# Expert-choice logits of a fused attention and mixture-of-experts kernel: rows stationary against gate weights stationary

## The chip, the cores and the metric

The kernel runs on one core of one Trainium2 chip. The metric is device microseconds (us) of one execution, as the median of several runs. All times below are in us unless marked ns.

## What is computed

Four batches of eight heads, 576 tokens and 64 elements a head go through an attention that keeps only scores within `tau` of the row's largest. The heads of a token are put side by side into a row of 512, which gives 2304 rows. Each row chooses one of 8 experts by the largest of 8 logits, the expert takes at most `capacity` rows in the order of the rows, and the row goes through that expert's two layers:

```python
x = attn_out.transpose(0, 2, 1, 3).reshape(2304, 512)
logits = x @ w_gate                       # 512 x 8
expert_idx = np.argmax(logits, axis=1)
probs = softmax(logits); gate_w = probs[i, expert_idx[i]]
disp[e, counts[e]] = x[i]                 # while counts[e] < capacity, rows in order
h = np.maximum(disp @ w1, 0); y = h @ w2  # w1: 512 x 1024, w2: 1024 x 512 for each expert
out[i] = gate_w[i] * y[expert_idx[i], pos[i]]
```

The change touches only `x @ w_gate` for the first 512 tokens of each batch.

## The kernel before

**Stages.** The attention runs over 16 pairs of heads (`s` in 0 to 15; `HH` = 4 pairs make one batch). Per pair TensorE (PE) computes the scores twice (`emit_s`, whose row maxima VectorE takes at L819, and `emit_d`, transposed, for the exponentials), ScalarE takes the exponentials (L880) and rounds them to f16 (L850), VectorE masks them (L884), GpSimd makes the low halves (L854), and PE multiplies by the values (`emit_av`, L900 and, for the 64 tail tokens of each head, L912) into the PSUM bank `xo`. GpSimd writes the scaled rows into `xr` (L950; tails into `xrt`).

**The gate.** When a pair's rows are there, `emit_xturn` transposes them, two blocks of 128 tokens at a time, into columns 0 to 255 of the PSUM bank `gp` (L955), and `emit_xturned` copies them with ScalarE into `xgt4` (L960). `xgt4` is carved out of the memory of `w2b`, and that is its name in the profile. It holds, for each of the four pairs `c` of a batch, 128 features by 512 tokens in f32. After the last pair of a batch `emit_logits` (L966) multiplies: for each of the 4 blocks of 128 tokens and each `c`, the 128x128 block of rows is the stationary operand and the 128x8 slice of the gate's weights `wg` moves. That is 16 matmuls a batch, and since the profile shows each f32 matmul as two passes with a weight load each, 32. The 64 tail tokens have their own path (`emit_turn` L981, `emit_turned` L987, `emit_logit` L997). Then `emit_gate1`, `emit_choice`, `emit_rank`, `emit_meta` and `emit_gate2` (L1021 to L1086) find expert and position on VectorE, with a few small matmuls, and GpSimd scatters the rows to DRAM (L1092).

**Experts.** The first rows of each expert ("early" tiles) are gathered before the last batch's rows are scattered, and the rest ("late") after it. Their layers are L377/L384 and L423, with weights loaded as `ws` and split into two f16 halves (L307/L314, L309 to L312).

**What sets the order.** No engine's order is written by hand. Every step is a task `T(key, engine, duration, function, dependencies, priority)`, and `Plan.run` simulates the engines with the written durations and emits the steps in the order that comes out. A task's duration and its dependencies thus move other tasks too. The logits of a batch were one task on PE, written as 1800 ns.

Of the kernel before, what the change touches and what calls it, by code (L numbers as in the profile page):

```python
# [14 lines left out]
AF = mybir.ActivationFunctionType  # L15
ALU = mybir.AluOpType
AX = mybir.AxisListType
# [3 lines left out]
P = 128  # L21
# [9 lines left out]
def view(ap, dims, offset=0):  # L31
    return bass.AP(tensor=ap.tensor, offset=ap.offset + offset, ap=[ap.ap[0]] + [list(d) for d in dims])
# [138 lines left out]
def attention_moe_kernel(ctx: ExitStack, tc: tile.TileContext, q, k, v, tau, w_gate, w1, w2, cap, out):  # L171
    nc = tc.nc
    B, H, S, D = q.shape
    NTOK, DM = out.shape
    E, _, F = w1.shape
    NJ = S // P
    TAIL = S - NJ * P
    NB = DM // P
# [27 lines left out]
    V = nc.vector  # L206

    def const_of(name, shape, dt=F32):
        return const.tile([P] + shape, dt, name=name)

    tau_t, g64, cap_f, cap_e = (const_of(n, [1]) for n in ("tau_t", "g64", "cap_f", "cap_e"))
    cap_i = const_of("cap_i", [2], I32)
    wg = const_of("wg", [NB, E])
    ntau = const_of("ntau", [1])
    ones, tri, tri2, ident16 = (const_of(n, [P], F16) for n in ("ones", "tri", "tri2", "ident16"))
    ident = const_of("ident", [P])
# [20 lines left out]
    for i, t0, m, pattern, base in (  # L237
# [4 lines left out]
        nc.gpsimd.iota(hs_i[:, i, t0:t0 + m], pattern=pattern, base=base, channel_multiplier=0)  # L242
    V.memset(ones, 1.0)
    V.memset(cum, 0.0)
    V.memset(zero, 0.0)
    nc.gpsimd.affine_select(
        out=tri, in_=ones, pattern=[[1, P]], base=0, channel_multiplier=-1, compare_op=ALU.is_gt, fill=0.0
    )
    for i in range(2):
# [6 lines left out]
        out=row_e, in0=desc, scalar1=-float(NTOK), scalar2=float(E * NTOK), op0=ALU.mult, op1=ALU.add  # L256
# [3 lines left out]
        out=more_e, in0=desc, scalar1=float(E - NP), scalar2=float(HP), op0=ALU.is_gt, op1=ALU.mult  # L260
# [4 lines left out]
        out=half[:, 1:2], in0=half[:, 0:1], scalar=-float(HP), in1=tok_l, op0=ALU.mult, op1=ALU.add  # L265
    )
    for t in (slice(0, NF), slice(NL, SLOTS)):
        V.tensor_scalar(out=hslot[:, 0, t], in0=hslot[:, 0, t], scalar1=half[:, 0:1], scalar2=None, op0=ALU.add)
    V.tensor_scalar(
        out=hslot[:, 2], in0=hslot[:, 0], scalar1=float(HP), scalar2=half[:, 1:2], op0=ALU.mult, op1=ALU.add  # L270
# [51 lines left out]
    psum = ctx.enter_context(tc.tile_pool(name="psum", bufs=1, space=PSUM))  # L322
    ps_x, ps_g = (psum.tile([P, 512], F32, name=n) for n in ("xo", "gp"))
# [119 lines left out]
    tb = {}  # L443
# [203 lines left out]
    if True:  # L647
# [14 lines left out]
        HH = H // 2  # L662
# [5 lines left out]
        def part(shape, dt=F32, i=1):  # L668
            n = 2 if dt == F32 else 1
            for d in shape:  # L670
                n *= d
            at[i] += n
            assert at[i] <= WB - 512
            v = wb[i][:, WB - at[i]:WB - at[i] + n]
            dims, step = [], 1
            for d in reversed(shape):
                dims.insert(0, [step, d])
                step *= d
            return view(v.bitcast(F32) if dt == F32 else v, dims)
# [5 lines left out]
        xgt4 = part([NB, NM])  # L685
# [273 lines left out]
        def emit_xturned(s, i):  # L959
            nc.scalar.activation(out=xgt4[:, s % HH, i * 2 * P:(i + 1) * 2 * P], in_=ps_g[:, 0:2 * P], func=AF.Copy)  # L960

        def emit_logits(b):
            gps[b, 0] = ps_g
            for j in range(NJ):
                for c in range(NB):
                    nc.tensor.matmul(  # L966
                        out=ps_g[:, 2 * P + j * E:2 * P + (j + 1) * E], lhsT=xgt4[:, c, j * P:(j + 1) * P], rhs=wg[:, c, :],
                        start=(c == 0), stop=(c == NB - 1),
                    )

        xgt, gps = {}, {}

# [16 lines left out]
        def emit_logit(b, j):  # L989
            gp = gps[b, j - j % NJ]  # L990
            xg = xgt.pop((b, j))
            o = 2 * P + (j % NJ) * E
            for c in range(NB):
                for z in range(1 if j < NJ else 2):
                    m = slice(0, P) if j < NJ else slice(z * TAIL, (z + 1) * TAIL)
                    x = xg[:, c] if j < NJ else xg[:, c % 2, c // 2 * TAIL:(c // 2 + 1) * TAIL]
                    nc.tensor.matmul(  # L997
                        out=gp[m, o:o + E], lhsT=x, rhs=wg[:, c, :], start=(c == 0), stop=(c == NB - 1)
                    )

        def bc(x, g, n):
# [122 lines left out]
        def emit_first2():  # L1124
# [10 lines left out]
        plan = Plan()  # L1135

        NU = 9 * NPR
        NQ = B * (NJ + 1)
# [3 lines left out]
            scat=13.88, ld=-34, lv=-26, sc=-25, hi=-24, lo=-22, tk=-20, s=-14, sj=0.8, m=-9, d=0, dj=1.8, e=-1.5, p=-1, h=.5, l=1, vs=-8, av=9, avx=4,  # L1142
# [4 lines left out]
        T, J = plan.add, plan.join  # L1147

        def last(kind, n, *more):
            return [(kind, n, *more)] if n >= 0 else []  # L1150
# [10 lines left out]
        T(("tau",), "V", 140, emit_tau, [("ltau",)], -60)  # L1161
        T(("lcap",), "S", 475, lambda: nc.sync.dma_start(out=cap_i, in_=cap.partition_broadcast(P)), [("s", 1, 3)], 20, dma=60, kind="load")
        T(("cap",), "V", 280, emit_cap, [("lcap",)], 25)
        T(("lwg",), "S", 475, lambda: nc.sync.dma_start(out=wg, in_=w_gate.rearrange("(c p) e -> p c e", p=P)), [("s", 1, 2)], 20, dma=230, kind="load")

        CUT = 2 * NJ + 3
        FIRST = 2
# [4 lines left out]
        for s in range(NPR):  # L1172
            b, a = divmod(s, HH)
            u = 9 * s
            scaled = s >= FIRST
            for is_q in (False, True):
                n = "q" if is_q else "k"
# [33 lines left out]
            for c in (0, 5, 1, 2, 3, 4):  # L1211
                pr = u + PR["d"] + PR["dj"] * (c % 5)
                n = 5 * s + c
                if c < 5:
                    free = [("p", *divmod(n - 2, 5))] if n >= 2 else []
                    if c:
                        m = 4 * s + c - 1 - N32
# [8 lines left out]
                if 0 < c < 5:  # L1226
                    m = 4 * s + c - 1 - N16
                    uses = [("av", m // 4, m % 4 // 2, j) for j in range(NJ)] if m >= 0 else []
                    T(("h16", s, c), "A", 1030, partial(emit_h16, s, c), [("p", s, c)] + uses, pr + PR["h"])
                    e = "V" if c in BY_V else "G"  # L1230
# [16 lines left out]
            t = u + PR["xt"] + PR["av"]  # L1247
# [7 lines left out]
                continue  # L1255
            n = u + 8
            t = n + PR["xt"]
            T(("logit", b, 0), "P", 1800, partial(emit_logits, b), [("xb", s, 1), ("lwg",)] + last("gate2", b - 1, NJ), t)
            qi = b * (NJ + 1) + NJ
            T(("ta", qi), "P", 216, partial(emit_turn, b, NJ, 0), [("xm", s - i, 2) for i in range(HH)] + [("xb", s, 1)], t)  # L1260
            T(("tb", qi), "A", 264, partial(emit_turned, b, NJ, 0), [("ta", qi)] + last("logit", b - 1, NJ), t, kind="psum")
            T(("logit", b, NJ), "P", 756, partial(emit_logit, b, NJ), [("tb", qi), ("gate2", b, 0)], t)
            for i in (0, NJ):
                t = n + PR["gate"]
# [21 lines left out]
        b = B - 2  # L1286
# [15 lines left out]
        def at(n):  # L1302
            return NU + PM["B0"] + n * PM["SL"]

        g = B - 1
        plan.urgent |= {(n, g, NJ) for n in ("gate1", "gexp", "choice", "rank", "meta", "gate2")} | {("scat", g, NJ, 0)} | {(n, NQ - 1) for n in ("ta", "tb")} | {("logit", g, 0), ("logit", g, NJ)}
        if PR["urg"] > 0:
            plan.urgent |= {(n,) for n in ("tot", "most", "left", "cnt", "cut", "alone", "lim", "base", "base2", "dv", "u", "w1", "w2")}
            plan.urgent |= {(n, 0) for n in ("ge", "pr", "sel", "row", "gix")}
# [26 lines left out]
        for i, t in enumerate((first, rest)):  # L1336
            m, p = t.stop - t.start, i / 2
# [29 lines left out]
        for t in range(NE, NS, GR):  # L1367
            m = min(GR, NS - t)
# [11 lines left out]
        for c in range(NCH):  # L1380
            ends = c == NCH - 1
            for i in range(2):
# [32 lines left out]
                for t in range(NS):  # L1415
                    early = t < NE and c == 0
                    n = NU + PR["early"] + t * PR["ej"] if early and i == 0 else at(pos)
                    o = (lambda p: n) if early and i == 0 else (lambda p: at(pos + PM[p]))
# [3 lines left out]
                    if i == 0:  # L1422
                        if c == 0:
                            xb = XB[t % len(XB)]
# [17 lines left out]
                        if t >= NE and (t % 2 or t == NS - 1):  # L1442
                            m = t % 2 + 1
# [3 lines left out]
                    else:  # L1447
# [3 lines left out]
                        e = "A" if c == 0 and t < NE else "V"  # L1451
# [74 lines left out]
```

## Time and profile before

| | |
|---|---|
| median of 3 runs | 625.91 (625.09 to 627.33) |
| the profiled execution's own time | 626.25 |
| its span, first to last instruction | 624.4 |
| mean granted TensorE clock | 0.959 |
| busy time in the span: PE, DVE, ACT, POOL | 556.9, 432.3, 383.3, 426.9 |

PE is TensorE, DVE is VectorE, ACT is ScalarE, POOL is GpSimd, PEld is PE's weight loads. A granted clock of 1.00 is 2.4 GHz and 0.50 is 1.2 GHz. Matmuls are pipelined and the ends of their rows are modelled, so what a group of them costs PE is read from its start to the start of the next. The four groups of logits start at 121.25, 198.46, 278.43 and 358.12; the first three lie inside the attention, the last one between attention and experts.

### The profile page before, as it was taken

The numbers are of one execution on the slowest core, as the hardware profiler recorded it, in microseconds if no ns is written. First come the engines' busy times: TensorE is split into PE (matmuls) and PEld (weight loads), VectorE is DVE, ScalarE is ACT, GpSimd is POOL, SyncE is SP. The second block draws the span as 40 slices with busy tenths as digits, with TensorE's granted clock in tenths as the row PEclk, the third lists the DMA queues.
The fourth block names the chain that finished last, engine by engine and source line by source line (L and its number), as shares of the span: only waits on it lengthen the run. The fifth ranks groups of instructions, "written<-read, shape, count | busy, mean of one in ns | idle before, by whom it ended". The sixth has DMA issues, their size and how long they took to land.

```text
span 624.4 us, 15985 instructions
## 1 busy us (share of the span) xinstructions
PE 556.9 (89%) x5990; PEld 378.3 (61%) x5990; DVE 432.3 (69%) x990; ACT 383.3 (61%) x523; POOL 426.9 (68%) x366
## 2 busy tenths in 40 slices
PE   0777999998999999999797895799999999999994
PEld 0234666765667666666566784665775577468652
DVE  4667988878886888886877869444555655555652
ACT  4359888878797688574467643448556645644410
POOL 5327887949887389772768536508788948886774
PEclk9989999989999899998798888989999999999997
DMA  5878777736677367662243845962579519861972
GB/s 152 193 174 166 135 149 138 152 95 156 152 171 137 58 172 133 116 87 49 77 141 99 296 160 157 223 157 77 203 194 220 173 67 222 207 202 61 232 185 100
DMA packets 171181, 94.26 MB, mean 151 GB/s; under 512 B 147027, under 2 KB 159383, under 8 KB 171098
## 3 DMA queue, kind: packets, MB, share of 16 engines
q1 hardware_dynamic: 157450, 50.47, 40.1%
q0 software_dynamic: 12352, 41.80, 20.8%
q8 instruction: 52, 0.85, 0.6%
q10 hardware_dynamic: 1296, 0.89, 0.4%
q14 instruction: 31, 0.25, 0.1%
HBM read 53.25 MB, written 10.24 MB: 102 GB/s over the span
## 4 chain that ended last, share of the span: by engine, by line
PE 60%; DVE 14%; DMA 9%; SPq 5%; ACT 4%; issue 4%; POOL 3%; ACTq 0%; POOLq 0%; DVEq 0%
PE b L384 10%; PE xo L900 9%; PE s L792 8%; PE d L792 7%; PE b L377 7%; PE xo L423 5%; PE gp L423 4%; PE b L423 4%; DVE w2b L884 3%; PE gp L966 2%; DMA out_dram<-latey,oix 2%; PE xo L912 2%; DVE mx L819 2%; SPq L733 2%; DMA qr<-in_q_dram 2%
## 5 line engine op out<-in xcount | busy, mean ns | idle before, releaser
L792 PE MATMUL s<-kT,qT 128*128 128x512 f16 (+2 forms) x576 | 99.5, 310 | 28.8 <-DMA kT<-kn 22.2
L819 DVE TENSOR_REDUCE mx<-s 128x1 f32<-128x512 f32 x144 | 94.4, 679 | 17.4 <-PE s L792 16.6
L792 PE MATMUL d<-qT,kT 128*128 128x512 f16 (+2 forms) x576 | 85.4, 302 | 6.0 <-DVE w2b L884 4.5
L384 PE MATMUL b<-w1b,latex 128*128 (+2 forms) x816 | 79.4, 274 | 5.3 <-DVE latex L359 3.6
L309 ACT ACTIVATE ws<-ws 128x1024 f32<-128x1024 f32 x48 | 50.5, 1051 | 51.1 <-DMA ws<-in_moe_w_dram 51.1
L384 PEld LDWEIGHTS <-latex 128*128 128x128 f16 (+1 forms) x816 | 62.3, 102 | 21.3 <-DVE latex L359 4.8
L792 PEld LDWEIGHTS <-qT 128*128 128x128 f16 (+1 forms) x640 | 39.7, 105 | 57.3 <-issue 25.7
L884 DVE SCALAR_TENSOR_TENSOR w2b<-d,ntau,w2b 128x1024 f32<-128x1024 f32 x56 | 71.0, 1276 | 3.6 <-ACT w2b L880 3.6
L854 POOL TENSOR_TENSOR p<-w2b,p 128x1024 f16<-128x1024 f32 x33 | 70.3, 2135 | 3.2 <-ACT p L850 2.8
L312 POOL TENSOR_TENSOR w2b<-ws,w2b 128x1024 f16<-128x1024 f32 x24 | 51.0, 2137 | 23.0 <-ACT w2b L310 22.8
L792 PEld LDWEIGHTS <-kT 128*128 128x128 f16 (+1 forms) x640 | 37.1, 102 | 47.7 <-issue 28.0
L312 POOL TENSOR_TENSOR w1b<-ws,w1b 128x1024 f16<-128x1024 f32 x24 | 51.3, 2141 | 20.6 <-ACT w1b L310 20.3
L880 ACT ACTIVATE w2b<-d 128x1024 f32<-128x1024 f32 x56 | 56.3, 1019 | 5.5 <-PE d L792 4.7
L900 PEld LDWEIGHTS <-p 128*128 128x128 f16 x1056 | 47.2, 103 | 14.8 <-issue 4.1
L377 PE MATMUL b<-earlyx,w1b 128*128 128x128 f16 x768 | 51.1, 228 | 5.4 <-DVE earlyx L359 5.2
L377 PEld LDWEIGHTS <-w1b 128*128 128x128 f16 x768 | 47.4, 102 | 12.8 <-issue 10.3
L900 PE MATMUL xo<-vH,p 128*128 128x65 f16 x704 | 49.9, 199 | 3.9 <-DVE rc L935 2.6
L423 PEld LDWEIGHTS <-lateh 128*128 128x128 f16 (+1 forms) x408 | 30.8, 103 | 33.6 <-issue 0.4
L296 POOL DMA_DIRECT2D ws<-in_moe_w_dram x50 | 37.3, 750 | 9.7 <-DVE w2b L314 7.3
L900 PE MATMUL xo<-vL,p 128*128 128x64 f16 x352 | 43.9, 197 | 0.0
L850 ACT ACTIVATE p<-w2b 128x1024 f16<-128x1024 f32 x33 | 34.8, 1055 | 6.1 <-DVE w2b L884 5.8
L310 ACT ACTIVATE w2b<-ws 128x1024 f16<-128x1024 f32 x24 | 25.4, 1057 | 20.9 <-PE gp L423 20.2
(231 smaller groups left out, 1225.6 us busy)
## 6 DMA issues: line engine op xcount, KB each, us to landing
ws<-in_moe_w_dram POOLq DMA_DIRECT2D x50, 512.0 KB, 5.1
ws<-in_moe_w_dram SPq DMA_DIRECT2D x14, 512.0 KB, 4.7
kr<-in_k_dram SPq DMA_DIRECT2D x15, 256.0 KB, 2.9
qr<-in_q_dram SPq DMA_DIRECT2D x14, 256.0 KB, 2.9
v<-in_v_dram SPq DMA_DIRECT2D x28, 128.0 KB, 3.2
qr<-in_q_dram ACTq DMA_DIRECT2D x2, 256.0 KB, 4.8
v<-in_v_dram POOLq DMA_DIRECT2D x4, 128.0 KB, 3.3
qT<-qn SPq DMA_TRANSPOSE x32, 4.7
```

Of the source, the lines that this page charges most:

```text
L296: eng.dma_start(out=t, in_=src)
L309: nc.scalar.activation(out=t, in_=t, func=AF.Copy, scale=W_SCALE)
L312: nc.gpsimd.tensor_tensor(out=dst[:, :, 1, :], in0=t, in1=dst[:, :, 0, :], op=ALU.subtract)
L377: nc.tensor.matmul(out=hp[:, f * P:(f + 1) * P], lhsT=wb[0][:, o:o + P], rhs=xT[t][:, xi], start=(d == 0 and z == 0), stop=(d == NB - 1 an ...
L384: nc.tensor.matmul(out=hp[m, 0:FC], lhsT=xT[t][:, xi, m], rhs=wb[0][:, bass.ds(r + (2 * d + wi) * FC, FC)], start=(d == 0 and z == 0), sto ...
L423: nc.tensor.matmul(out=yp[m], lhsT=h[:, o, hi, m], rhs=wb[1][:, bass.ds(r + wi * DM, DM)], start=(z == 0), stop=(z == len(ops) - 1),)
L792: nc.tensor.matmul(out=out, lhsT=l, rhs=r, start=(z == 0), stop=(z == 1), **kw)
L819: V.tensor_reduce(out=m[:, i, 0:1], in_=ps_s[i % 2], axis=AX.X, op=ALU.max)
L854: eng.tensor_tensor(out=p[:, 1], in0=p32_of(s, k), in1=p[:, 0], op=ALU.subtract)
L880: nc.scalar.activation(out=t, in_=d, func=AF.Exp, scale=sc_s)
L884: V.scalar_tensor_tensor(out=t, in0=d, scalar=ntau, in1=t, op0=ALU.is_ge, op1=ALU.mult)
L900: nc.tensor.matmul(out=ps_x[:, j * DV:j * DV + r.shape[-1]], lhsT=l, rhs=r, start=(z == 0), stop=(z == len(ops) - 1))
```

## The change

The operands are exchanged. For each half `h` of a batch (256 tokens), `emit_gated` makes the gate's slices stationary: `wg` is now 128 x 4 x 32, zero but for the 8 experts, and each `c` has a column tile of its own, 32 columns wide, with its output in 32 partitions of `gp`. The rows move, 256 columns at a time. The four parts of the sum then lie in four groups of partitions, tokens along the row. `emit_parts` copies them (128x256) back to SBUF on ScalarE, over `xgt4`'s first block. `emit_logits` adds the four parts and turns them in one matmul per 128 tokens, with the parts stationary and `pick` moving, a 128x8 matrix of 0 and 1. `pick` is made once from the identity; `wg` is filled with zeros once. The tail's transposes (`ta`) now wait for the second copy, since both use columns 0 to 255 of `gp`.

```diff
-    wg = const_of("wg", [NB, E])
+    wg = const_of("wg", [NB, P // NB])
+    pick = const_of("pick", [E])
...
+    V.memset(wg, 0.0)
...
-        def emit_logits(b):
+        def emit_gated(b, h):
             gps[b, 0] = ps_g
-            for j in range(NJ):
-                for c in range(NB):
-                    nc.tensor.matmul(
-                        out=ps_g[:, 2 * P + j * E:2 * P + (j + 1) * E], lhsT=xgt4[:, c, j * P:(j + 1) * P], rhs=wg[:, c, :],
-                        start=(c == 0), stop=(c == NB - 1),
-                    )
+            for c in range(NB):
+                r = slice(c * P // NB, (c + 1) * P // NB)
+                nc.tensor.matmul(
+                    out=ps_g[r, 0:2 * P], lhsT=wg[:, c, :], rhs=xgt4[:, c, 2 * h * P:2 * (h + 1) * P], start=True, stop=True
+                )
+
+        def emit_parts(b, h):
+            nc.scalar.activation(out=xgt4[:, 0, 2 * h * P:2 * (h + 1) * P], in_=ps_g[:, 0:2 * P], func=AF.Copy)
+
+        def emit_logits(b, h):
+            for j in (2 * h, 2 * h + 1):
+                nc.tensor.matmul(
+                    out=ps_g[:, 2 * P + j * E:2 * P + (j + 1) * E], lhsT=xgt4[:, 0, j * P:(j + 1) * P], rhs=pick,
+                    start=True, stop=True,
+                )
...
-                        out=gp[m, o:o + E], lhsT=x, rhs=wg[:, c, :], start=(c == 0), stop=(c == NB - 1)
+                        out=gp[m, o:o + E], lhsT=x, rhs=wg[:, c, 0:E], start=(c == 0), stop=(c == NB - 1)
...
+        T(("pick",), "V", 100, lambda: V.tensor_reduce(
+            out=pick, in_=view(ident[:, 0:E], [[1, E], [P // NB, NB]]), axis=AX.X, op=ALU.add), [("tau",)], 25)
...
-            T(("logit", b, 0), "P", 1800, partial(emit_logits, b), [("xb", s, 1), ("lwg",)] + last("gate2", b - 1, NJ), t)
+            for h in range(2):
+                T(("lgt", b, h), "P", 560, partial(emit_gated, b, h), [("xb", s, 1), ("lwg",)] + ([("lge", b, 0)] if h else []), t + h / 4)
+                T(("lge", b, h), "A", 370, partial(emit_parts, b, h), [("lgt", b, h)], t + h / 4, kind="psum")
+                T(("lgs", b, h), "P", 520, partial(emit_logits, b, h), [("lge", b, h), ("pick",)] + last("gate2", b - 1, NJ), t + h / 4)
+            J(("logit", b, 0), [("lgs", b, 0), ("lgs", b, 1)])
...
-            T(("ta", qi), "P", 216, partial(emit_turn, b, NJ, 0), [("xm", s - i, 2) for i in range(HH)] + [("xb", s, 1)], t)
+            T(("ta", qi), "P", 216, partial(emit_turn, b, NJ, 0), [("xm", s - i, 2) for i in range(HH)] + [("lge", b, 1)], t)
```

How the steps fall on the engines is shown at three places. In the changed kernel every line number is higher (`emit_gated` is L968, `emit_parts` L973, `emit_logits` L977).

PE at the logits of the first batch, before:

```order
L792 MATMUL s_145<-kT_181,qT_184 128x512
L966 MATMUL gp<-wg,w2b 128x8 x16
L981 MATMUL gp<-ident,xrt 128x128 x2
L792 LDWEIGHTS kT_183
L792 MATMUL gp<-qT_186,kT_183 64x64
```

The same place in the change, with the pieces that lie between:

```order
L968 MATMUL gp<-w2b,wg 32x256 x4
L794 LDWEIGHTS kT_185
L794 MATMUL gp<-qT_188,kT_185 64x64
...
L902 MATMUL xo<-v_170,w1b 128x65
L977 MATMUL gp<-pick,w2b 128x8 x2
L968 MATMUL gp<-w2b,wg 32x256 x4
L794 LDWEIGHTS qT_186
L794 MATMUL s_148<-kT_183,qT_186 128x512
...
L992 MATMUL gp<-ident,xrt 128x128 x2
L977 MATMUL gp<-pick,w2b 128x8 x2
```

The block of 16 has become four pieces, with one block of `emit_av` between the first two and two blocks and a pair of score matmuls between the last two. In all four batches the order is of this kind.

ACT at the same place, in the change (`w2b<-gp` at L962 is the last transposed block, at L973 the two new copies; `kn` and `qr` are the next pairs' keys and queries):

```order
L962 ACTIVATE w2b<-gp 128x256
L882 ACTIVATE w2b<-d_150 128x1024
L973 ACTIVATE w2b<-gp 128x256
L882 ACTIVATE c_192<-gp 128x64
L747 ACTIVATE kn_178<-kr_174 128x2x9x64
L739 ACTIVATE qr_176<-qr_176,g_72 128x576
L973 ACTIVATE w2b<-gp 128x256
L747 ACTIVATE qn_182<-qr_176 128x18x64
L998 ACTIVATE xgT<-gp 128x256
```

Before, the exponential, `kn`, `qr` and `xgT` stood here in a row; the two copies now stand among them, one behind the exponential and one behind `qr`.

PE at the logits of the last batch, in the change (`b` and `earlyx`, `earlyy`, `earlyh` belong to the early tiles of the experts, L379 being their first layer; `oh,tri` opens `emit_rank`):

```order
L968 MATMUL gp<-w2b,wg 32x256 x4
L353 MATMUL b_4866<-ident,earlyy 128x128 x4
...
L977 MATMUL gp<-pick,w2b 128x8 x2
L968 MATMUL gp<-w2b,wg 32x256 x4
L379 LDWEIGHTS w1b
L379 MATMUL b_4869<-earlyx,w1b 128x128
...
L992 MATMUL gp<-ident,xrt 128x128 x2
L977 MATMUL gp<-pick,w2b 128x8 x2
L353 MATMUL b_4867<-ident,earlyy 128x128 x4
...
L1061 MATMUL gp<-oh,tri 128x8
```

Between the first and the third piece stand four transposes and 24 matmuls of L379, between the third and the fourth 24 more. Before the rank's first matmul there are eight transposes and six matmuls of L425 now, where there were 24 matmuls of the first layer and four transposes.

## Rows read from the trace of the kernel before

**Rows 1.** Page, part 4: the chain that ended last, by engine
```profile
PE 60%; DVE 14%; DMA 9%; SPq 5%; ACT 4%; issue 4%; POOL 3%; ACTq 0%; POOLq 0%; DVEq 0%
```

**Rows 2.** Timeline of PE, first batch's logits: start, duration, engine, line, operation
```profile
121.25 3.63 PE L966 MATMUL gp<-wg,w2b 128*128 128x8 f32 x32
124.74 0.42 PE L981 MATMUL gp<-ident,xrt 128*128 128x128 f32 x2
```

**Rows 3.** Windows, PE alone: stretch and length, PE busy, granted clock, DMA
```profile
126.40:129.81 3.41, 3.41 (x34) 0.50 0.24 76
...
201.49:208.32 6.83, 6.38 (x45) 0.50 0.14 43
...
283.41:286.82 3.41, 3.41 (x34) 0.50 0.00 0
...
361.92:365.33 3.41, 3.41 (x30) 0.50 0.16 59
```

**Rows 4.** Windows: stretch, length, busy PE, PEld, DVE, ACT, POOL, clock, DMA
```profile
65.00:115.00 50.00, 49.79 (x651) 33.90 (x650) 43.98 (x92) 43.86 (x63) 41.99 (x34) 1.00 0.74 144
118.00:146.00 28.00, 25.77 (x313) 18.37 (x311) 22.03 (x69) 20.77 (x34) 18.71 (x16) 0.94 0.63 154
197.00:225.00 28.00, 25.28 (x275) 17.86 (x272) 20.30 (x64) 18.38 (x29) 15.07 (x14) 0.88 0.58 124
276.50:304.50 28.00, 25.22 (x305) 17.94 (x303) 21.84 (x60) 14.07 (x23) 15.57 (x12) 0.93 0.43 92
```

**Rows 5.** Timeline of PE: f32 passes with 65 moving columns
```profile
116.93 0.63 PE L912 MATMUL xo<-v,w2b 128*64 128x65 f32 x8
117.40 0.28 PE L912 MATMUL xo<-v,c 128*64 128x65 f32 x2
```

**Rows 6.** Timeline of PE: four passes of 512 columns on two column tiles
```profile
90.39 0.62 PE L792 MATMUL s<-kT,qT 128*64 128x512 f16 x4
90.95 0.82 PE L792 MATMUL d<-qT,kT 128*128 128x512 f16 x3
```

**Rows 7.** Timeline of PE behind the first batch's logits
```profile
125.27 0.20 PE L900 MATMUL xo<-vH,w1b 128*128 128x65 f16 x1
...
125.90 0.59 PE L792 MATMUL s<-kT,qT 128*128 128x512 f16 x2
...
128.67 1.06 PE L792 MATMUL s<-kT,qT 128*64 128x512 f16 x4
```

**Rows 8.** Timeline of ACT at the first batch's logits
```profile
120.95 1.02 ACT L880 ACTIVATE w2b<-d 128x1024 f32<-128x1024 f32 x1
121.85 1.17 ACT L745 ACTIVATE kn<-kr 128x1152 f16<-128x1152 f32 x1
122.91 0.78 ACT L737 ACTIVATE qr<-qr,g 128x576 f32<-128x576 f32 x1
```

**Rows 9.** Line L960: duration min/median/max in ns, first and last start
```profile
L960 ACT ACTIVATE w2b<-gp x32: 364/384/402, 68.7 to 356.3; 128x256 f32<-128x256 f32 x32
```

**Rows 10.** Timeline of PE around the last batch's logits
```profile
354.97 0.63 PE L955 MATMUL gp<-ident,xr 128*128 128x128 f32 x2 [1.70 <-ACT w2b L960]
...
358.12 3.88 PE L966 MATMUL gp<-wg,w2b 128*128 128x8 f32 x32
361.86 0.63 PE L981 MATMUL gp<-ident,xrt 128*128 128x128 f32 x2
...
365.52 0.17 PE L1050 MATMUL gp<-oh,tri 128*128 128x8 f16 x1
...
365.87 0.64 PE L351 MATMUL b<-ident,earlyy 128*128 128x128 f32 x4
...
367.74 0.64 PE L997 MATMUL gp<-wg,xgT 128*64 128x8 f32 x16
...
369.61 1.50 PE L377 MATMUL b<-earlyx,w1b 128*128 128x128 f16 x24
```

**Rows 11.** Chain of waits in order of time, before the last batch
```profile
345.30 7.00 DMA ws<-in_moe_w_dram
```

More of the change, by code (lines that the diff above doesn't have):

```diff
@@ L1163, in attention_moe_kernel @@
         T(("cap",), "V", 280, emit_cap, [("lcap",)], 25)
-        T(("lwg",), "S", 475, lambda: nc.sync.dma_start(out=wg, in_=w_gate.rearrange("(c p) e -> p c e", p=P)), [("s", 1, 2)], 20, dma=230, kind="load")
+        T(("pick",), "V", 100, lambda: V.tensor_reduce(
+            out=pick, in_=view(ident[:, 0:E], [[1, E], [P // NB, NB]]), axis=AX.X, op=ALU.add), [("tau",)], 25)
+        T(("lwg",), "S", 475, lambda: nc.sync.dma_start(out=wg[:, :, 0:E], in_=w_gate.rearrange("(c p) e -> p c e", p=P)), [("s", 1, 2)], 20, dma=230, kind="load")
         CUT = 2 * NJ + 3
@@ L1305, in attention_moe_kernel @@
         g = B - 1
-        plan.urgent |= {(n, g, NJ) for n in ("gate1", "gexp", "choice", "rank", "meta", "gate2")} | {("scat", g, NJ, 0)} | {(n, NQ - 1) for n in ("ta", "tb")} | {("logit", g, 0), ("logit", g, NJ)}
+        plan.urgent |= {(n, g, NJ) for n in ("gate1", "gexp", "choice", "rank", "meta", "gate2")} | {("scat", g, NJ, 0)} | {(n, NQ - 1) for n in ("ta", "tb")} | {(n, g, h) for n in ("lgt", "lge", "lgs") for h in range(2)} | {("logit", g, NJ)}
         if PR["urg"] > 0:
```

## The prediction

> **What bounds the kernel now.** I read the chain of waits first. PE holds 60% of it and DVE 14% [rows 1]; no other engine comes near, so time on PE counts, and DVE sets how much of a gain survives. The second view is PE's timeline at the first batch's logits. The 32 passes begin at 121.25 and the next instruction at 124.74 [rows 2]: 3.49 us, or 109 ns for a pass that moves only 8 columns. What is paid there is the loading of 128x128 f32 weights, 32 times. The third view is the granted clock. After every one of the four groups of logits it falls to 0.50, the lower level of 1.2 GHz: at 126.40, 201.49, 283.41 and 361.92, for 3.41 us (6.83 the second time) [rows 3]. PE was never idle in the first of these groups, so it isn't a wait that precedes the fall, but 3.5 us of passes with almost no moving columns. The fourth view is the busy time by stretch. In the steady part of the attention (65 to 115) DVE is busy 43.98 of 50, or 0.88; in 28 us that begin some 2 us ahead of each of the first three groups it is busy 22.03, 20.30 and 21.84 [rows 4]. At the steady pace that work takes 25.0, 23.1 and 24.8 us. So 3.0, 4.9 and 3.2, together 11.1 us, are lost around the logits of the attention. The last group is another matter and is costed by itself.
>
> **The gate's weights as stationary operand.** A pass moves 256 f32 columns now. The nearest rows are the f32 passes with 65 columns: eight of them start within 0.47 us (116.93 to 117.40), 59 ns each [rows 5], so at most 0.90 ns a column and 0.23 us for 256. Four column tiles with two passes each take two passes, 0.46, if the tiles run side by side, and eight, 1.85, if not. For two column tiles the trace has an answer: four passes of 512 columns, which one after the other would take 0.85 at a column per cycle of 2.4 GHz, hold PE 0.56 (90.39 to 90.95) [rows 6]. I take 0.46, as this row is nearest, and keep 1.85 for the range. The same row leaves 0.13 us beyond the 0.43 of two passes, in which the tile width changes; I count 0.1 for each such change, four a batch. The Trainium skill ("TensorEngine Tiling (Array Packing)", Key Properties) says that changing the tiling mode drains the engine; rows 6 agree with some 0.1 us of it.
>
> **The product with `pick`.** Two matmuls a half are four passes of the old kind, 4 x 0.109 = 0.44. PE's new cost for a batch is 2 x (0.46 + 0.44) + 0.4 = 2.2, against 3.49: **1.3 saved**. The serial bound gives 5.0, 1.5 lost.
>
> **The clock.** What PE did before each fall is gone from the program; between the pieces stand blocks of `emit_av` and score matmuls, work with which the clock stays at 1.00 from 65 to 115 [rows 4]. So I expect no fall after the logits. Work done at half clock takes half the time: 1.7, 3.2 (6.38 busy) and 1.7 in the three batches [rows 3]. The bound on the other side is no gain at all. Together PE gets ahead by 3 x 1.3 + 6.6 = **10.5 us** over three batches.
>
> **The copies and the two new waits.** A copy of 128x256 takes 0.38 [rows 9], eight of them 3.0 us, on an engine that is busy 14 to 21 of 28 us here [rows 4]; that cost is nothing where PE has other work. I walked the first batch. First piece 121.25 to 121.8; the tail scores and one block of `emit_av` (0.63, from 125.27 to 125.90 [rows 7]) hold PE until 122.65. ACT's exponential ends at 121.97 [rows 8], the copy at 122.35, so `pick` needn't wait. Second products at 123.1, second piece until 123.8. Before PE needs the second copy it has a pair of score matmuls (0.43) and two blocks (1.26), until 125.45. ACT has the small exponential, `kn` (1.17) and `qr` (0.78) ahead of that copy [rows 8] and ends it near 124.9. Transposes and `pick` then end at 126.2, where PE stood at 128.67 before [rows 7]: 2.5 us ahead, which is what the terms above give by that point. What waits behind `pick` on PE, if ACT is later, is everything; what waits on ACT behind a copy is `qn` or `c`, and DVE on those. The tail's transposes wait for the second copy and come 1 us later than before, off the chain, since the gate's first part is worked on then.
>
> **What of it reaches the end.** At most the 11.1 us that DVE loses. At least what PE's lead exceeds its idle time in the same stretches (28 minus 25.77, 25.28 and 25.22, together 7.7 [rows 4]): 10.5 - 7.7 = 2.8. Between 2.8 and 11.1 I take **6.0**, under the middle because the gate's chain of small DVE instructions, which also thins those stretches, stays.
>
> **The last batch.** Before, the logits run from 358.12 to 361.86, and the rank, behind 24 matmuls at half clock, starts at 365.52 [rows 10]. Now: first piece with its change of width 0.56, four transposes 0.5, 24 matmuls 1.4 (1.50 with the last one's tail at 369.61), `pick` 0.44, second piece 0.56, 24 matmuls 1.4, transposes 0.3, `pick` 0.44: the logits are there at 363.7, 1.9 later. The eight transposes and six matmuls ahead of the rank take about 2.3 (0.5 and 1.87, from 365.87 to 367.74), so the rank starts near 366.0, 0.5 later; the tail's logits follow it by 24 matmuls, near 367.8, as before (367.74). I count **0**, with 1 us of gain and, if the clock falls all the same, 2.8 us of loss (2 x 1.4) as bounds.
>
> **The rest.** One more fill and one small reduction on DVE lie at the start, where the first transfers are waited for; the load of the gate's weights moves the same pieces. The planner's new durations also shift score matmuls, copies and a few loads by some places all over the program. I see no reason for a sign and count 0, with 2 us either way.
>
> **Sum.** 626.25 (the profiled execution's own time; span 624.4) - 6.0 = 620.25. That execution lies 0.34 above the median, so I forecast **619.9**. About 0.3%, 1.9 us, is what a measurement of this kernel can tell from no change.
>
> **Rivals.**
> - *Strict order of passes.* The two passes of a matmul stand one behind the other. If a tile's second pass holds back the next tile's first, a half takes five passes, 1.15, not two. PE's new cost is 3.6 and only the clock's 6.6 (minus 0.3) is left; at the same share (6.0 of 10.5) that is 3.6 and **622.3**; fully serial tiles give 1.2 and 624.7. Rows 6 don't decide it, as their passes alternate between tiles. The Trainium skill speaks for this rival ("TensorE: Matmul & The Clock Gate", Part 3): matmuls start and end in program order and only weight loads are pulled ahead. No row here shows four tiles. Chance 0.17.
> - *The clock falls all the same.* A quarter of the passes of 8 columns remains (8 of 32 a batch), and what of the old stretch brought the fall about isn't told apart by these rows. Then 3.9 x 0.57 = 2.2 is left: **623.7**. Against it: the clock is 1.00 in all of 65 to 115 [rows 4], with many short passes. Chance 0.10.
> - *The copies come late (slower).* PE stops at each `pick` until ACT has made a copy, and ACT works in order, with instructions of 1.02 and 1.17 ahead of it [rows 8]. The like handover in the last batch, the transposes behind a copy, held PE 1.70 [rows 10]. It decides from a mean stop of 6.0/8 = 0.75 us at each of the eight copies. At 1.05, one ACT instruction, 8.4 goes and the time is **628.3**. For it: ACT's order there is fixed by durations that the planner only assumes. Against it: the walk above. Chance 0.13.
> - *The gain is given back before the experts.* The chain passes through a 7.00 us load of weights ahead of the last batch [rows 11]. If that load starts no earlier, nothing of the first three batches' gain arrives: **625.9**. Against it: the load follows DVE's work on the one before. Chance 0.08.
> - *All of it arrives*: 11.1, **614.8**. Chance 0.05.
>
> **Numbers.** The forecast has 0.47. Faster by over 0.3% are nearly all of it, most of the strict order, half of the falling clock, and the last rival: 0.73. Same: 0.14, mostly the load. Slower: 0.13, the copies. The range reaches from the last rival to beyond the load's case, 614.5 to 626.5, and leaves out the late copies.
>
> **What would show it.** Right: four passes of two tiles or more starting within a few ns and a piece of 256 columns in about 0.5; PE at clock 1.00 for 10 us after each of the first three groups; DVE over 23 of 28 there; no stop at `pick` over 0.5. Wrong: pieces of 1.1 or more; clock 0.50 behind them; PE idle with ACT's copy as releaser; a weights load before the last batch that starts where it did.

## The result and the profile after

The forecast was 619.9 with a range of 614.5 to 626.5. Measured: 629.37 as the median of 20 runs (625.25 to 634.09), beside 624.98 for the kernel before (20 runs, 616.8 to 631.28) on the same chip: **a ratio of 1.011, 95% interval 1.007 to 1.014**. The change made the kernel slower by about 1%, and the time lies outside the range. Medians here and below are over all runs, while a ratio leaves out the runs more than 1.5% above the fastest of their kernel, so the two can differ, most of all for the kernel before beside the first four experiments, where a single time of 615.65 leaves three of eleven in. The profiled execution took 632.51, with a span of 630.8 and a mean clock of 0.967.

Page, part 1, of the changed kernel (busy time by engine), and the first line of part 4 (the chain that ended last, by engine):

```profile
PE 548.9 (87%) x5958; PEld 366.8 (58%) x5958; DVE 432.9 (69%) x992; ACT 386.3 (61%) x531; POOL 426.7 (68%) x366
...
PE 57%; DMA 14%; DVE 13%; issue 6%; ACT 4%; SPq 3%; POOL 3%; POOLq 0%; ACTq 0%; DVEq 0%
```

PE is busy 8.0 less than before (556.9), as was wanted, and yet the span is 6.4 longer. (These are single executions: the same changed kernel has 555.0 of busy PE in e4 below.) In the chain, DMA has gone from 9% [rows 1] to 14%. First the place that was changed. The timeline of PE at the first batch's logits in the changed kernel, which answers to [rows 2]:

```profile
129.27 0.64 PE L968 MATMUL gp<-w2b,wg 128*32 128x256 f32 x8
129.84 0.25 PE L794 MATMUL gp<-qT,kT 128*64 128x64 f16 x4
...
130.68 0.61 PE L977 MATMUL gp<-pick,w2b 128*128 128x8 f32 x4
131.22 0.64 PE L968 MATMUL gp<-w2b,wg 128*32 128x256 f32 x8
131.80 0.61 PE L794 MATMUL s<-kT,qT 128*128 128x512 f16 x2
```

Eight passes of 256 columns take 0.57, from 129.27 to 129.84: four column tiles run side by side. The windows of 10 us from the start of each group of logits show busy PE, PEld, DVE, ACT and POOL, then the granted clock, DMA share and GB/s:

```profile
129.30:139.30 10.00, 9.90 (x151) 7.09 (x151) 7.84 (x22) 8.21 (x15) 4.92 (x5) 1.00 0.61 145
...
204.00:214.00 10.00, 7.64 (x100) 4.90 (x97) 5.46 (x13) 6.31 (x12) 5.20 (x5) 1.00 0.51 110
...
287.00:297.00 10.00, 9.17 (x136) 6.37 (x136) 6.98 (x21) 4.46 (x10) 2.72 (x2) 1.00 0.51 84
364.00:374.00 10.00, 9.99 (x143) 8.02 (x142) 7.31 (x29) 7.72 (x18) 0.00 (x0) 0.98 0.53 165
```

The clock stands at 1.00 behind the first three groups and at 0.98 behind the last; before, it fell to 0.50 behind all four [rows 3]. So the mechanism that the forecast named is there, right behind the logits. But the first group starts at 129.27, and before it started at 121.25 [rows 2]. **Eight microseconds are lost ahead of the first instruction that the change touches.** The chain of waits in order of time, up to there:

```profile
76.71 6.49 DMA qT<-qn
...
121.97 5.24 DMA qT<-qn
```

Neither piece stands in the chain of the kernel before. The transposes of queries and keys by DMA (`qn` to `qT`, `kn` to `kT`, issued by SP) take longer. The view of a tile gives min/median/max in ns, the time that an issue holds SP's queue, before:

```profile
L779 SPq DMA_TRANSPOSE qT<-qn x16: 1849/2343/3642, 12.1 to 278.1; - x16
L774 SPq DMA_TRANSPOSE kT<-kn x16: 1877/2210/3199, 14.2 to 272.9; - x16
```

and after:

```profile
L781 SPq DMA_TRANSPOSE qT<-qn x16: 2657/2818/5777, 11.2 to 287.8; - x16
L776 SPq DMA_TRANSPOSE kT<-kn x16: 2474/2758/3763, 14.1 to 282.0; - x16
```

The shortest of 16 has gone from 1.85 to 2.66. The same view has a third row, 16 transposes of half of `qn`, whose issue takes 1.24 at least on both sides; their landing tells instead. Before (L784) and after (L786), in us from the issue:

```profile
DMA to landing us min/median/max: 2.8/2.9/4.7
...
DMA to landing us min/median/max: 3.2/3.3/5.2
```

Nothing in the diff names a transpose. What it does is enlarge `wg` from 128 to 512 bytes in each partition and add `pick`, 32 bytes, and both are allocated ahead of nearly everything on that side of SBUF. `w1b`, `w2b`, `ws`, `kr`, `qr`, `kn`, `qn`, `kT1` and `qT1`, among others, all move up by 416 bytes. In the compiled program before, `kn0` stands at byte 111104 and `qn0` at 120320, both multiples of 512.

### The profile page after: what moved, and what is told of

Its sections match the earlier page's. It is cut to its first block, busy times and chain, and to the rows that moved or that the text cites. A ratio compares the mean times of both kernels' runs of the same rounds, so it can differ in the third digit from the quotient of the medians.

```text
span 630.8 us, 15931 instructions
## 1 busy us (share of the span) xinstructions
PE 548.9 (87%) x5958; PEld 366.8 (58%) x5958; DVE 432.9 (69%) x992; ACT 386.3 (61%) x531; POOL 426.7 (68%) x366
## 3 DMA queue, kind: packets, MB, share of 16 engines
q1 hardware_dynamic: 157450, 50.47, 44.3%
## 4 chain that ended last, share of the span: by engine, by line
PE 57%; DMA 14%; DVE 13%; issue 6%; ACT 4%; SPq 3%; POOL 3%; POOLq 0%; ACTq 0%; DVEq 0%
PE b L386 10%; PE xo L902 8%; PE s L794 7%; PE d L794 7%; PE b L379 6%; PE xo L425 4%; PE b L425 4%; PE gp L425 4%; DMA qT<-qn 2%; DMA kT<-kn 2%; DMA out_dram<-latey,oix 2%; PE xo L914 2%; DVE w2b L886 2%; DMA qr<-in_q_dram 2%; DMA latey<-xd,gix 2%
## 5 line engine op out<-in xcount | busy, mean ns | idle before, releaser
L794 PE MATMUL s<-kT,qT 128*128 128x512 f16 (+2 forms) x576 | 97.8, 306 | 36.5 <-DMA kT<-kn 25.3
L425 PEld LDWEIGHTS <-lateh 128*128 128x128 f16 (+1 forms) x408 | 30.8, 103 | 33.7 <-issue 0.6
L379 PEld LDWEIGHTS <-w1b 128*128 128x128 f16 x768 | 44.9, 99 | 7.9 <-issue 4.5
L379 PE MATMUL b<-earlyx,w1b 128*128 128x128 f16 x768 | 48.8, 222 | 0.4 <-DVE earlyx L361 0.2
L952 POOL TENSOR_TENSOR xr<-xs,rc 128x256 f32<-128x256 f32 x32 | 19.9, 623 | 27.1 <-DVE rc L938 13.6
```

The source lines that it names most:

```text
L379: nc.tensor.matmul(out=hp[:, f * P:(f + 1) * P], lhsT=wb[0][:, o:o + P], rhs=xT[t][:, xi], start=(d == 0 and z == 0), stop=(d == NB - 1 an ...
L425: nc.tensor.matmul(out=yp[m], lhsT=h[:, o, hi, m], rhs=wb[1][:, bass.ds(r + wi * DM, DM)], start=(z == 0), stop=(z == len(ops) - 1),)
L794: nc.tensor.matmul(out=out, lhsT=l, rhs=r, start=(z == 0), stop=(z == 1), **kw)
```

## Experiments

The theory: the transposes are slower because their source (`kn`, `qn`) no longer stands at a multiple of some power of two. The rivals: the new steps themselves or their order, or other moved buffers. Ratios are to the kernel before, beside which each was run on one chip; that kernel's medians there were 628.4 (first four), 634.9 (next four) and 625.9 (last four), so times of different groups aren't compared.

**The move without the change, and the change without the move.** Four kernels, two of them the kernel before with padding, two the changed kernel:

```diff
-    wg = const_of("wg", [NB, E])
+    wg = const_of("wg", [NB * E + 104])[:, 0:NB * E].rearrange("p (c e) -> p c e", e=E)
```

(e1; `+ 112` in e3), and in the changed kernel (e2; e4 is unchanged):

```diff
-    pick = const_of("pick", [E])
+    pick = const_of("pick", [E + 24])[:, 0:E]
```

> The kernel before with 416 bytes more behind wg in every partition and nothing else, so that the buffers behind it (weights, staging, kr, qr, kn, qn, kT1, qT1) start 32 bytes past a multiple of 64 instead of on one, as in the change. Placement theory: transfers get slower as in the change (queue q1 44% instead of 40% of the engines' span, 138624 packets of 256 bytes) and the time rises by 8 to 12 us, to 632 to 637. Rival, the new order and the copies cost the time: the same as before, 622 to 628. Rival, the profiled execution met a slow chip: the same as before.

> The change with 96 bytes more behind pick, so that the same buffers are moved by 512 bytes in all and start on multiples of 64 again. Placement theory: q1 back to 40%, and the gain at the logits shows: 617 to 622, 3 to 8 us under before and some 10 under the change. Rival, order and copies: as the change, 627 to 632. Rival, slow chip: as the change on the same chip.

> Control: the kernel before with everything behind wg moved by 448 bytes, a multiple of 64 but not of 128. Placement theory with 64 bytes as the step: the same as before, 622 to 628, q1 at 40%. If it is any move, or a step of 128 or more, that costs: 630 or more.

> The change once more, on the chip of the other three. Placement theory and order-and-copies theory: 627 to 632, about 1.01 times before, q1 at 44%. Slow-chip theory: 617 to 623, q1 at 40%.

| | median | ratio (95%) |
|---|---|---|
| e1: before, moved by 416 | 640.52 | 1.030 (1.017 to 1.044) |
| e3: before, moved by 448 | 640.09 | 1.031 (1.022 to 1.041) |
| e4: change as it was (416) | 630.64 | 1.015 (1.006 to 1.023) |
| e2: change, moved by 512 | 610.13 | 0.983 (0.974 to 0.993) |

The move alone costs the kernel before 12.2 by the medians (640.52 - 628.37) and 19 by the ratio, and undoing it gives the changed kernel 20.5 (630.64 - 610.13). At either place the change is a gain: where the buffers stand at multiples of 512 it is 18.2 by these medians and 1.7% by the ratio (16.8 and 2.6% in e9, below, beside more runs of the kernel before), where they don't it is 9.9 (640.52 - 630.64). The directions were expected, the sizes weren't: e1 was put at 632 to 637 and e2 at 617 to 622. That 448 would do was a miss: a step of 64 bytes isn't it.

**How far, and which buffers.** e5 and e12 are e2 with `E + 56` and `E + 88`, moves of 640 and 768 bytes. e6 is the change as it was (416) with

```diff
+        deadp.tile([P, 24], F32, name="gap")
         kns = [deadp.tile([P, 2, KB, P], F16, name=f"kn{i}") for i in range(NKN)]
```

which puts `kn`, `qn`, `kT1` and `qT1` back to multiples of 512 and leaves `w1b`, `w2b`, `ws`, `kr` and `qr` off. e7 is the reverse: e2 with a gap of 104 elements there. e8 is e2 with `hw`, the source of the late transposes, moved to a multiple of 512:

```diff
+            ctx.enter_context(tc.tile_pool(name="gap", bufs=1, side="right")).tile([P, 88], F32, name="gap")
             pools["hr"] = ctx.enter_context(tc.tile_pool(name="hr", bufs=HR, side="right", reuse_waits="tile"))
```

> The changed kernel with everything behind `pick` moved by 640 bytes in all: 128 beyond a multiple of 512. Theory A, only a multiple of 512 bytes serves the transposes as they stood: time as of the unmodified change, ratio to before 1.01, an isolated transpose of one half of `qn` 1.5 us. Theory B, 128 bytes is enough (448 bytes, an odd multiple of 64, was not): as with 512 bytes, ratio 0.975 to 0.985, an isolated transpose 1.2 us.

> The changed kernel with a gap of 96 bytes between the raw queries `qr` and the first `kn`: only `kn`, `qn`, `kT1`, `qT1` stand at multiples of 512 again, everything else (`w1b`, `w2b`, `ws`, `kr`, `qr`) stays 416 bytes off. Theory A, the sources of the transposes carry the cost: ratio to before 0.975 to 0.99, start of the first logits at 120 to 122, an isolated transpose 1.2 us. Theory B, loads or the reads of PE, DVE and ACT from the moved buffers carry it: ratio 1.005 to 1.02, first logits at 128 to 130.

> The reverse: the changed kernel moved by 512 bytes in all, and a gap of 416 bytes ahead of the first `kn`, so that only `kn`, `qn`, `kT1`, `qT1` are off. Theory A (sources of the transposes): ratio 1.00 to 1.02, first logits at 128 to 130, transposes 1.5 us. Theory B (the other buffers): ratio 0.975 to 0.99, first logits at 120 to 122.

> The changed kernel moved by 512 bytes in all, and a gap of 352 bytes on the other side that brings `hw`, the source of the 28 late transposes `lateh<-hw`, from 352 beyond a multiple of 512 to a multiple. If the source's place is the cause for every transpose, these get shorter: a sixth to a quarter off the median of the landing, and 0 to 4 us off the end, so 606 to 610 where the version without this gap has 610 (ratio 0.970 to 0.983). If it is a matter of `kn` and `qn` alone, the transposes keep their time and the ratio is 0.98.

> The changed kernel with everything behind `pick` moved by 768 bytes, 256 beyond a multiple of 512. If a multiple of 256 is enough for the transposes' sources: ratio 0.965 to 0.985 like the yardstick, an isolated transpose 1.2 us. If it takes 512: ratio 0.995 to 1.015, an isolated transpose 1.5 us, as with 128, 416 and 448.

| | median | ratio (95%) |
|---|---|---|
| e5: moved by 640 | 635.78 | 1.002 (0.998 to 1.006) |
| e6: only the transposes' buffers put back | 614.04 | 0.970 (0.964 to 0.975) |
| e7: only the transposes' buffers off | 632.46 | 0.997 (0.994 to 1.001) |
| e8: 512, and `hw` at a multiple | 616.24 | 0.971 (0.965 to 0.977) |
| e12: moved by 768 (last group) | 609.71 | 0.974 (0.971 to 0.978) |

e6 and e7 settle which buffers it is: 18.4 lies between them, nearly the 20.5 between e4 and e2. Against the expectations e6 gains a little more (0.975 to 0.99 was written), and e5 and e7 lose a little less (1.01, and 1.00 to 1.02). The other moved buffers cost nothing that can be seen: e6, where they are off, is as fast as e8 beside it, where they aren't. The order of instructions on each of the five engines is the same in the change, e2, e7 and e12. And the other work on `kn` and `qn` keeps its length, so it is not their writing that pays: ACT fills a `kn` in 1154 ns in the change (L747) and 1155 in e9, and POOL makes the low halves (L754) in 1279 and 1278. The same rows as above, for e7:

```profile
L782 SPq DMA_TRANSPOSE qT<-qn x16: 2661/2801/5402, 11.2 to 288.9; - x16
L777 SPq DMA_TRANSPOSE kT<-kn x16: 2509/2748/3718, 14.1 to 283.1; - x16
```

for e6:

```profile
L782 SPq DMA_TRANSPOSE qT<-qn x16: 1872/2102/5202, 11.3 to 274.1; - x16
L777 SPq DMA_TRANSPOSE kT<-kn x16: 1901/2113/3306, 13.4 to 269.1; - x16
```

and for e12:

```profile
L781 SPq DMA_TRANSPOSE qT<-qn x16: 1839/2296/5089, 11.2 to 270.0; - x16
L776 SPq DMA_TRANSPOSE kT<-kn x16: 1966/2201/3310, 13.3 to 265.0; - x16
```

Three readings. A multiple of 256 is enough (e12), 128 isn't (e5), nor 416 or 448. The source decides, not the destination: the 16 transposes of a row go in turn into `qT0`, `qT1` and `qT2`, and in e7 only `qT1` had moved, yet the shortest of all 16 is 2.66; and `qT0` and `qT2` stand at 480 beyond a multiple of 512 in every version, also in those that gain: in e6 all 16 half transposes land within 2.8, whichever of the three they go into. The other rows of DMA barely tell it: queue q1 holds 40.1% of the engines before and 44.3% after, but 42.6% in e2, which gains.

The packets on queue q1 tell it directly. A transpose of half of `qn` whose packets run without a gap mostly takes 1.17 to 1.21 from the start of its first 256-byte packet to that of its last with the source at a multiple of 256 bytes (before, e6, e9, e12), and 1.52 to 1.58 without, nearly the same 128 (e5), 416 (the change, e1, e7) and 448 (e3) bytes beyond a multiple of 512.

And a miss: aligning `hw` (e8) gave nothing over e6 beside it, where 0 to 4 had been expected over e2. It isn't that these late transposes don't pay. Those of 1024 packets that start 1.17 to 1.18 after their issue and run without a gap take 1.38 to 1.39 in e9, with `hw` off (at 398.49, 402.15, 406.19 and 582.05), and 1.07 in e8 (at 561.08 and 585.29). But most of the 28 wait or are interrupted and take longer in both, and of the 0.3 saved on a few of them nothing is seen at the end.

**Where the well-placed change gains.** It gains 16.8 (e9, which is e2 again, as the yardstick; 18.2 in e2) where the forecast had 6.0. e10 is the kernel before with only the written duration of its logits changed:

```diff
-            T(("logit", b, 0), "P", 1800, partial(emit_logits, b), [("xb", s, 1), ("lwg",)] + last("gate2", b - 1, NJ), t)
+            T(("logit", b, 0), "P", 3500, partial(emit_logits, b), [("xb", s, 1), ("lwg",)] + last("gate2", b - 1, NJ), t)
```

e11 is e2 with the old products in the new arrangement: each half's `emit_gated` does eight matmuls 128x8 as before, `emit_logits` does nothing, and the copies are made for nobody. Its `lgt` tasks also wait for the gate of the batch before, as the one task of logits did. Apart from these products the order on PE, and on the other engines, is that of e2.

```diff
-            for c in range(NB):
-                r = slice(c * P // NB, (c + 1) * P // NB)
-                nc.tensor.matmul(
-                    out=ps_g[r, 0:2 * P], lhsT=wg[:, c, :], rhs=xgt4[:, c, 2 * h * P:2 * (h + 1) * P], start=True, stop=True
-                )
+            for j in (2 * h, 2 * h + 1):
+                for c in range(NB):
+                    nc.tensor.matmul(
+                        out=ps_g[:, 2 * P + j * E:2 * P + (j + 1) * E], lhsT=xgt4[:, c, j * P:(j + 1) * P], rhs=wg[:, c, 0:E],
+                        start=(c == 0), stop=(c == NB - 1),
+                    )
```

> The changed kernel with everything behind `pick` moved by 512 bytes once more, as the yardstick for the runs beside it on this chip. Expected: ratio to before 0.965 to 0.985, first logits at 119.5 to 121.5.

> The kernel before with the written duration of the logits task as 3500 ns instead of 1800, the time that its trace shows for the group (3.49 us). Only the order that comes out of it changes; no buffer moves. Theory A, the gain of the well-placed change is PE's time and clock at the logits: ratio 0.995 to 1.005. Theory B, much of it is a better order because the written durations are now true: ratio 0.975 to 0.99.

> The well-placed changed kernel with its split, its copies, its waits and its written durations, but with the old products in the place of the new ones: eight matmuls 128x8 a half with rows stationary, and no product with `pick` (the copies are still made, nobody reads them). PE's order is that of the changed kernel otherwise. Theory A (products): PE has 1.3 us more in each batch and the clock falls behind the logits again; ratio 0.985 to 1.005, that is 8 to 16 us above the yardstick. Theory B (order, split): within 4 us of the yardstick, ratio 0.970 to 0.985.

| | median | ratio (95%) |
|---|---|---|
| before | 625.86 | 1 |
| e10: before, duration 3500 | 622.87 | 0.995 (0.992 to 0.998) |
| e11: new arrangement, old products | 619.01 | 0.989 (0.985 to 0.993) |
| e9: change, moved by 512 | 609.11 | 0.974 (0.970 to 0.977) |

So of the well-placed change's 16.8, the products are 9.9 (619.01 - 609.11), and the arrangement alone (two halves with other work between them, new durations) is 6.9. A truer duration without the split gives 3.0 (e10, at the edge of its theory A); what else of the arrangement makes up the 6.9 wasn't taken apart. In e11 the size of theory A holds (9.9, of 8 to 16 above the yardstick) and the 4 us of theory B doesn't, but the arrangement's 6.9 stands beside it: both parts are real. Windows of 28 us from about 2 us ahead of the first three groups, as in [rows 4], for e11 (DVE is the third busy time):

```profile
117.10:145.10 28.00, 24.80 (x286) 18.43 (x286) 20.30 (x64) 18.78 (x30) 16.53 (x15) 0.88 0.64 143
195.80:223.80 28.00, 25.53 (x334) 18.82 (x331) 23.45 (x70) 21.31 (x36) 17.90 (x16) 0.96 0.67 139
275.00:303.00 28.00, 24.94 (x300) 17.16 (x297) 23.58 (x71) 15.55 (x26) 15.22 (x12) 0.94 0.39 87
```

and for e9:

```profile
118.00:146.00 28.00, 24.63 (x328) 16.47 (x327) 24.77 (x72) 22.99 (x37) 20.69 (x17) 1.00 0.83 184
193.50:221.50 28.00, 25.53 (x337) 17.48 (x333) 24.71 (x71) 21.91 (x36) 19.14 (x16) 0.93 0.70 158
270.70:298.70 28.00, 25.39 (x324) 16.05 (x323) 24.85 (x74) 16.70 (x28) 16.06 (x13) 0.94 0.40 86
```

DVE does 64.2 us of work in the three windows before [rows 4], 67.3 in e11 and 74.3 in e9. That is 24.8 of 28, or 0.88, the pace of the undisturbed attention: nothing of DVE's time is lost around the logits any more. At that pace the products' 7.0 us of DVE work are worth 8.0, most of the 9.9.

## Why the prediction was wrong, step by step

**Where PE's lead and losses sit.** Starts of the four groups of logits, from PE's timelines, with the span:

| | first | second | third | fourth | span | fourth to end |
|---|---|---|---|---|---|---|
| before | 121.2 | 198.5 | 278.4 | 358.1 | 624.4 | 266.3 |
| e1 (before, off) | 128.8 | 212.0 | 294.4 | 374.0 | 638.2 | 264.2 |
| change | 129.3 | 204.0 | 287.0 | 364.0 | 630.8 | 266.8 |
| e4 (change again) | 129.8 | 204.8 | 290.9 | 367.4 | 629.1 | 261.7 |
| e11 | 119.5 | 197.3 | 276.9 | 353.9 | 615.3 | 261.4 |
| e9 | 120.4 | 195.0 | 272.6 | 345.9 | 607.1 | 261.2 |

**The failed step is "The rest".** It reads: "the load of the gate's weights moves the same pieces", and "I see no reason for a sign and count 0, with 2 us either way". It went through instructions and durations and not through memory. Put off 256, the buffers cost the change 20.5 (e4 against e2); the text has no term for it, and no rival. It is also what tips the sign: without it the ratio is 0.974 to 0.983. With the two parts of the gain the account closes: 20.5 lost, less 9.9 and 6.9 gained, is 3.7 slower, beside 4.4 measured (629.37 - 624.98). Where does it arrive? Page, part 5, the scores on PE in the changed kernel (count, busy and mean ns, idle time before them and what ended most of it):

```profile
L794 PE MATMUL s<-kT,qT 128*128 128x512 f16 (+2 forms) x576 | 97.8, 306 | 36.5 <-DMA kT<-kn 25.3
```

and in e9:

```profile
L794 PE MATMUL s<-kT,qT 128*128 128x512 f16 (+2 forms) x576 | 98.0, 306 | 25.6 <-DMA kT<-kn 21.1
```

Of the 23.7 between the two spans, 10.9 are idle time ahead of the scores; PE's idle time in all grows by 18.6 (81.9 against 63.3, span less busy time), and the rest is PE's busy time (548.9 against 543.8). How 0.8 us on a transpose becomes a piece of 6.49 in the chain wasn't isolated.

The Trainium skill has the rule that the forecast should have weighed ("DMA: Bandwidth & Descriptors", How a descriptor splits into AXI transactions): a transaction must start at a multiple of 256 bytes, so a descriptor that starts elsewhere pays for bytes that it doesn't want. The step of 256 is what e5 and e12 show. The size isn't: by that rule a piece of 256 bytes would need 12, 13 or 14 beats of 32 bytes in place of 8 at the places of e5, the change and e3 (an estimate from the page's figure), but half of `qn` takes 1.3 times as long in all three (1.54 to 1.18). Nor is it spread over all pieces: of queue q1's 256-byte packets of the first 345 us 8.9% take over 30 ns in the change, against 1.0% before, while the median stays 18 ns.

**The same step was wrong a second time**, in the other direction: the order that comes out of the new durations and the split was to be worth 0, with 2 either way, and is worth 6.9 (e11).

**The products: right, and their price too.** A piece of 256 columns was put at 0.46 + 0.1 and takes 0.57; the product with `pick` at 0.44 and a change of width, and takes 0.54 (130.68 to 131.22). The strict order of passes, at 1.15 a piece or more, is refuted. It leaned on the rule of the Trainium skill ("TensorE: Matmul & The Clock Gate", Part 3) that matmuls start and end in program order. In the compiled program the two passes of a matmul stand next to each other; in e2 four passes start 7 ns apart (120.129 to 120.149) and the other four 0.24 behind them (120.369 to 120.389). The rows don't name the tile of a pass. If the first four are one of each tile, which the 0.57 of the whole piece speaks for, the second pass of a tile does not hold back the next tile's first, and the rule doesn't hold here across column tiles.

**The clock: right behind the logits, and not the end of the falls.** In the change and in e9 the 10 us behind each of the first three groups are at 1.00 (behind the last 0.98 and 0.92). But in e9 the clock falls again 22 us behind the second group:

```profile
217.40:224.20 6.80, 6.49 (x63) 5.10 (x62) 4.75 (x9) 2.96 (x5) 6.11 (x4) 0.52 0.80 165
```

In e11, with the old products, it falls at once only behind the first group (0.53 over 122.00 to 128.80), but 24 us behind the second (0.53 over 221.00 to 227.80) and 23 behind the third (0.53 over 299.50 to 306.30). So the stretch from the first group to the fourth is the fairer measure, before, in e11 and in e9:

```profile
121.25:358.12 236.87, 218.50 (x2713) 155.56 (x2712) 191.10 (x448) 168.20 (x252) 170.36 (x138) 0.94 0.56 130
...
119.46:353.93 234.47, 217.90 (x2712) 156.00 (x2712) 191.04 (x447) 169.89 (x257) 170.04 (x138) 0.94 0.55 131
...
120.43:345.86 225.43, 207.56 (x2689) 143.64 (x2688) 190.63 (x448) 170.06 (x257) 169.62 (x137) 0.97 0.56 136
```

The split alone (e11) shifts single falls but leaves the mean at 0.94; with the new products it is 0.97. By these means the time at 1.2 GHz falls by some 15 us, worth half of that, about 7 (an estimate), near the forecast's 6.6. It is one execution of each, and the same stretch has 0.95 in the change and 0.92 in e4, which is the same kernel; so the clock's share of the gain isn't settled.

**What of it reaches the end: undersized.** Taken: 6.0 of 10.5, "under the middle because the gate's chain of small DVE instructions, which also thins those stretches, stays". e9's windows show no thinning left, and the products are worth 9.9. The upper bound of the step, 11.1, was the better number.

**The copies: right where placed well.** In e9 nobody waits for the two copies of a batch. In the change as it was, the tail's transposes wait 3.2 in all for two of them (`PE gp L992`, longest 2.4), still not `pick`. The rival of the late copies would have given 628.3, near the time measured, and is wrong all the same: e2 has the same copies in the same order on every engine and takes 610. Here the nearness is luck.

**The last batch: nothing against it.** It was counted as 0. From the start of the fourth group to the end e9 takes 261.2 and e11, with the old products, 261.4. The kernel before takes 266.3, but two executions of the change differ by as much (266.8, and 261.7 in e4), so a gain of 5 there can't be told from none.

**The weights load before the experts: not a limit.** In e9 the piece `ws<-in_moe_w_dram` of the chain starts at 333.85, against 345.30 before [rows 11], so it moves with the rest.

**The bound of 0.3%** was too small: single runs of the kernel before lie between 616.8 and 631.28, and 20 runs of each kernel gave an interval of 0.35% to either side.

## What to carry to other kernels

A diff that changes the size of an early buffer moves every buffer behind it, and that can cost more than the change gains: compare the addresses of all buffers before and after, not only the instructions. Here the sources of DMA transposes wanted multiples of 256 bytes, so pad small constants until the pool behind them stands as it stood, or put the gap right ahead of the buffers that need it. When a profile after is slower, look first at the last point that the change can't have touched: a loss there isn't the change's own work, and one run with padding tells the two apart.

## What the runs showed of the hardware that was not expected

The same 16 transposes from SBUF to SBUF (`qT<-qn`) hold SP's queue for at least 1.84 to 1.87 with their source at a multiple of 256 bytes, and for at least 2.62 to 2.66 from 128, 416 or 448 bytes beyond a multiple of 512 (e5; e1, e4, e7 and the change; e3). Without a gap a transpose of half of `qn` mostly moves its packets in 1.17 to 1.21 and 1.52 to 1.58. The place of the destination shows no effect (0 and 480 beyond a multiple of 512 in e6). Four 32-column tiles of f32 matmuls, eight passes of 256 columns, take 0.57, where two such passes were estimated at 0.46. The best version here is the change with 24 unused elements behind `pick`: 609.11 against 625.86, a ratio of 0.974 (0.970 to 0.977).
